# Gates of two routing groups in one pass behind the second list, constants and checks on other engines or later, u-term sums behind the mask

## The chip, the cores and the metric

The kernel runs on one core of a Trainium2 chip. The metric is the device time of one execution in microseconds (us); lower is better. A core has five engines, each with its own instruction stream: TensorE (PE, with its weight loads shown apart as PEld), VectorE (DVE), ScalarE (ACT), GpSimd (POOL) and SyncE (SP). They wait for one another by semaphores, and 16 DMA engines move the data.

## The reference

What is computed is a linear attention (4 batches, 8 heads, 768 steps, head size 48), whose output rows go through a mixture of 8 experts, two of them per token:

```python
for t in range(S):
    cur = np.einsum('bhd,bhe->bhde', u[None] * kt, vt)
    y[:, :, t] = np.einsum('bhd,bhde->bhe', rt, state + cur)
    state = w[None, :, :, None] * state + np.einsum('bhd,bhe->bhde', kt, vt)
x = y.transpose(0, 2, 1, 3).reshape(3072, 384)
noisy_logits = x @ w_gate + np.log1p(np.exp(x @ w_noise)) * noise
top2 = np.argpartition(-noisy_logits, 2, axis=1)[:, :2]
top2_w = softmax of the two logits, with 1e-9 in the denominator
for e in range(8):
    for k in range(2):
        mask = top2[:, k] == e
        h = np.maximum(x[mask] @ w1[e], 0.0)
        out[mask] += top2_w[mask, k, None] * (h @ w2[e])
```

Shapes of the experts: w1 is 8 x 384 x 1024, w2 is 8 x 1024 x 384, all float32.

## The kernel before

**Attention.** The 3072 tokens are 24 tiles of 128, i = chunk * 4 + batch. The loop `for i in range(NT)` writes each engine's stream in this order: `products(i)` puts the elementwise products on POOL (rku of tile i+1, L410 and L414, from tile 13 on L421 alone; kd of tile i+2, L402; the state's product z, L511); `ystate`, `kvup` and `yout` are matmuls into py and RV; `zup_v` folds RV into the state on DVE (z, L504 and L507); `uterm_b(i+1)` makes the "u-term" of the next tile on DVE: c, the sum of rku over a head (a reduce, L444; from tile 13 a copy, L442, of sums that PE makes from rku at L433 in the tile before), and, up to tile 8 (`CV_DVE`), cv = v * c (L448); `xout(i)` makes the tile's output x = py + cv (L560); `turn_kr(i+2)` transposes k and r on PE into KX and RV (L225), from which ACT makes kT (L462) and DVE rT (L464); `scores(i+1)` is 16 matmuls into PAB (L476); `turn_x(i)` transposes x (L225); and `mask(i+1)` makes am from PAB on DVE (L484, two instructions). RV is one buffer: the state's sums of tile i must have been read by z before `turn_kr(i+2)` may write it, and rT must have been read before the next sums.

**Routing.** Tiles 0 to 11 are group 0, tiles 12 to 23 group 1. `route(g)` turns a group's logits into the two chosen experts, each token's slot in its expert's list and its gates. It is a generator whose small DVE instructions are let in between the tiles by `steps` and `tick`: group 0 within tiles 13 to 23, group 1 within the first part of the expert stage. `drop` builds two operands on DVE (r_oa, r_ob) and queues a `place`, a set of matmuls (RT, L709) that scatters token numbers into a list; its `lag` says how many matmuls of the expert stage go ahead of it. `rows` turns the list L into gather indices (lt, lt, GR; L883 to L885), and `xgather` fetches the rows by indirect DMAs that POOL issues (L1020). `expneg` with the tag "r2" is a polynomial for exp, some 12 DVE instructions on 128 x 12 elements per group (L591 to L605); the gates follow (L842 to L854) and are written to DRAM by SP (xd<-r_a), from where the GT gathers read them. Within tiles 20 to 23, POOL also splits expert weights into high and low parts (w1l, L356 and L359).

**Experts.** Each list tile goes through ph = x w1 (L1131) and pym = h w2 (L1167), with every float32 matmul as three reduced-precision ones. `s` counts chunks of list tiles; `tile_counts` runs at s = 2.

**What sets the order.** The Python order above is each engine's instruction order; nothing is reordered later. A tile pool's buffer is free when its last reader is done.

Of the kernel before, what the change touches and what calls it, by code (L numbers as in the profile page):

```python
# [56 lines left out]
def kernel(  # L57
# [524 lines left out]
    def expneg(a, shape, tg, res):  # L582

        def T(nm, dt=F32):
            t = rtp[0].tile([128, GB * (E if len(shape) == 3 else 1)], dt, name=tg + nm, bufs=1)
# [83 lines left out]
    def drop(g, mm2, ej2, ijv, w_, c0, first):  # L669
# [29 lines left out]
        late_mm.append([2, lambda: place(n, parts, pL),  # L699
# [19 lines left out]
    def rest(g):  # L719
# [3 lines left out]
        for c in pairs(g, SLI[:, :, i0:i1], SL[g], "d"):  # L723
            yield 0.2
        mm2, ej2 = c
# [3 lines left out]
    GATES, list0 = {}, []  # L729

    def route(g, lists=True, behind=iter(())):
# [17 lines left out]
        for j, _ in enumerate(expneg(a, sh, "r1", ee)):  # L749
            if j == 1:  # L750
                nc.vector.tensor_add(zp, P(0, sh), gt)
            next(behind, None)
# [21 lines left out]
        for _ in behind:  # L774
            yield
# [3 lines left out]
        da, e2 = T("da", [128, n]), T("e2", [128, n])  # L779
# [24 lines left out]
        ex = expneg(da, [128, n], "r2", e2)  # L804
# [31 lines left out]
        if not lists:  # L836
            yield from slots(g, ex)
        def gates():
            for _ in ex:
                yield  # L840
            dn = GTS[:, 1, i0:i1]
            nc.vector.tensor_scalar(dn, e2, 1.0, 1e-9, op0=ALU.add, op1=ALU.add)  # L842
            yield
            gts = GTS[:, :, i0:i1]
            nc.vector.reciprocal(gts[:, 0], dn)
            yield
            nc.vector.tensor_mul(gts[:, 1], e2, gts[:, 0])
            yield
            if lists:
                og = T("os", [128, 2, n, E])  # L850
                nc.vector.tensor_mul(og, oh, gts[:, :, :, None].to_broadcast([128, 2, n, E]))
                yield 0.3
                gd = T("a")
                nc.vector.tensor_add(gd, og[:, 0], og[:, 1])  # L854
                while g and not list0:
                    yield "wait"
                nc.sync.dma_start(xd[i0 * 128:i1 * 128, DM:].rearrange("(n p) e -> p n e", p=128), gd)
                yield 0.25

        GATES[g] = gates()  # L860
        if not lists:
            yield from GATES[g]
        if lists:
# [23 lines left out]
    def tokens(a, b):  # L887
# [4 lines left out]
        f1 = const.tile([128, E * NJ], F32, name="f1")  # L892
# [123 lines left out]
    def xgather(e, ci, early_=-1):  # L1016
        for t in chunks(e)[ci]:
# [307 lines left out]
    for i in range(NT):  # L1325
        products(i)
        if early_done and (0, 0) not in XG:
            xgather(0, 0, 0)
        if i + 5 < NT:
            load(i + 5, (0, 2))  # L1330
        if i in (4, 6):
            next(flag)
        if NZ_AT <= i < NZ_AT + B:
            load_nz(i - NZ_AT)
        if i == B:
# [15 lines left out]
        if i and i + 1 < NT:  # L1351
# [6 lines left out]
        if i == I_EARLY and (0, 0) not in XG:  # L1358
            xgather(0, 0, 0)
        if i == NT - 1:  # L1360
            logits_out(i - 1)
            route_when_done(i - 1)
            steps(3)
            xT_first(lambda: turn_x(i))
            p1a = p1(0, 0)
        else:
# [11 lines left out]
            if not i:  # L1378
# [3 lines left out]
        if not i:  # L1382
# [87 lines left out]
    for s in range(1, len(seq)):  # L1470
# [96 lines left out]
        if s == 2:  # L1567
            tile_counts(CAP)
# [11 lines left out]
    with tc.If(any_r > 0):  # L1580
        bad_r = nc.values_load(tab[:, E:E + 1], min_val=0, max_val=1)
        with tc.If(bad_r > 0):
# [13 lines left out]
            nc.vector.memset(ie_n[:, 0, 0:1], 0.0)  # L1596
# [60 lines left out]
```

## Time and profile before

| | |
|---|---|
| median of 3 runs | 589.64 us (589.39 to 593.2) |
| the profiled execution | 589.92 us |
| its span, first to last instruction | 588.2 us |
| PE busy | 568.2 us (97%) |
| DVE / ACT / POOL busy | 348.1 (59%) / 284.5 (48%) / 280.0 us (48%) |
| mean granted clock of TensorE | 0.995 |
| chain that ended last | PE 89%, DVE 5%, POOL 2%, issue 2% |

The span is 1.72 us shorter than the profiled execution's time, and that execution is 0.28 us above the median. PE's share of 97% is a mean over two stages: the attention, up to about 128 us of the span, in which other engines hold PE at some places, and the experts behind it, in which PE is nearly always busy. In the rows below a time in brackets is the idle time of the engine before that instruction and what ended it. [...]

### The profile page before, as it was taken

Reading aid. Unit: us, or ns where it says so; the run is one execution under the profiler, and the core shown is the slowest. Engines: PE = TensorE matmul, PEld = TensorE weight load, DVE = VectorE, ACT = ScalarE, POOL = GpSimd, SP = SyncE. Lnnn points to the kernel's source line nnn. Section 1 sums busy time; section 2 is a strip of 40 time slices with the busy share of each in tenths; the row PEclk is TensorE's granted clock in tenths of the full one; section 3 lists DMA queues with packets and bytes.
Section 4 is the critical chain, followed back from the end, with each engine's and each line's share of the span. In section 5 each row is a group of like instructions: output and inputs, shape, how many; then the busy total and the mean of one; then the engine's idle time right before and its main releaser. Section 6 shows DMA issues by size and latency. Waiting matters only on the chain.

```text
span 588.2 us, 13907 instructions
## 1 busy us (share of the span) xinstructions
PE 568.2 (97%) x5383; PEld 543.4 (92%) x5384; DVE 348.1 (59%) x788; ACT 284.5 (48%) x712; POOL 280.0 (48%) x416
## 2 busy tenths in 40 slices
PE   8899899989999999999999999999999999999995
PEld 5799888879989999999999999999999999999995
DVE  7998698888864544556454554546363546454331
ACT  4348766842363624455445444454454455445220
POOL 8999455740336443436345453434262436423222
PEclk9999999989999999999999999999999999999999
DMA  8999889258405644765655646365845546424211
GB/s 166 224 219 205 201 202 210 83 142 258 125 35 189 184 131 120 189 138 175 108 154 164 177 116 200 98 184 127 173 118 153 169 127 187 124 82 85 67 35 42
DMA packets 143225, 86.53 MB, mean 147 GB/s; under 512 B 118624, under 2 KB 133215, under 8 KB 143152
## 3 DMA queue, kind: packets, MB, share of 16 engines
q1 hardware_dynamic: 132368, 56.76, 40.3%
q0 software_dynamic: 10160, 28.81, 16.0%
q8 instruction: 44, 0.72, 0.5%
q14 instruction: 29, 0.24, 0.1%
q10 hardware_dynamic: 624, 0.00, 0.1%
HBM read 58.81 MB, written 19.86 MB: 134 GB/s over the span
## 4 chain that ended last, share of the span: by engine, by line
PE 89%; DVE 5%; POOL 2%; issue 2%; ACT 1%; DMA 1%; POOLq 0%; ACTq 0%
PE ph L1131 37%; PE pym L1167 34%; PE py L531 4%; PE PAB L476 3%; PE pym L1160 2%; PE pym L1158 2%; PE KX L225 2%; PE py L569 1%; DVE am L484 1%; PE RV L494 1%; POOL kd L402 1%; PE RV L225 1%; PE RV L182 1%; PE RT L709 1%; PE ptm L1049 1%
## 5 line engine op out<-in xcount | busy, mean ns | idle before, releaser
L1167 PE MATMUL pym<-w1h,hb 128*128 128x384 f32 x768 | 200.3, 337 | 0.0
L1137 DVE SCALAR_TENSOR_TENSOR hb<-ph,hb 128x384 fp32r<-128x384 f32 x128 | 71.1, 556 | 116.7 <-ACT ht L1135 74.2
L1167 PEld LDWEIGHTS pym<-w1h,hb 128*128 128x128 f32 x768 | 139.3, 188 | 0.2
L1131 PE MATMUL ph<-xh,w0h 128*128 128x384 f32 (+1 forms) x384 | 136.0, 354 | 0.0
L1131 PE MATMUL ph<-xh,w0l 128*128 128x384 f32 (+1 forms) x384 | 135.6, 353 | 0.0
L1131 PE MATMUL ph<-xl,w0h 128*128 128x384 f32 (+1 forms) x384 | 130.4, 353 | 0.0
L1167 PE MATMUL pym<-w1l,hb 128*128 128x384 f32 x384 | 129.2, 336 | 0.0
L1135 ACT ACTIVATE hb<-ph 128x384 fp32r<-128x384 f32 x128 | 62.9, 492 | 106.7 <-PE ph L1131 106.7
L1192 POOL DMA_INDIRECT out_dram<-ot,TK x56 | 60.1, 1073 | 97.2 <-DVE ot L1186 42.1
L1020 POOL DMA_INDIRECT xg<-xd,GR x56 | 62.0, 1107 | 49.2 <-DVE r_e L603 24.4
L1131 PEld LDWEIGHTS ph<-xh,w0h 128*128 128x128 f32 x384 | 72.6, 189 | 3.5
L1131 PEld LDWEIGHTS ph<-xh,w0l 128*128 128x128 f32 x384 | 72.6, 189 | 3.1
L1131 PEld LDWEIGHTS ph<-xl,w0h 128*128 128x128 f32 x384 | 72.5, 189 | 3.2
L1035 POOL DMA_INDIRECT pv<-out_dram,GA x49 | 50.3, 1026 | 52.4 <-DMA out_dram<-ot,TK 39.7
L1167 PEld LDWEIGHTS pym<-w1l,hb 128*128 128x128 f32 x384 | 72.1, 188 | 0.1
L1105 ACT ACTIVATE xh<-xj 128x384 fp32r<-128x384 f32 (+1 forms) x42 | 21.1, 502 | 43.3 <-DVE xj L1103 43.1
L1175 ACT ACTIVATE ot<-pym 128x384 f32<-128x384 f32 x42 | 20.4, 486 | 39.9 <-PE pym L1167 33.1
L1106 DVE TENSOR_TENSOR xl<-xj,xh 128x384 fp32r<-128x384 f32 (+1 forms) x42 | 22.5, 535 | 24.8 <-ACT xh L1105 24.8
L1091 ACT ACTIVATE pl<-xg 128x768 uint16<-128x768 uint16 (+1 forms) x42 | 35.3, 841 | 1.4 <-DMA xd<-pl 1.4
L484 DVE TENSOR_TENSOR am<-PAB,mneg 128x512 int32<-128x512 int32 x48 | 30.8, 682 | 4.9 <-PE PAB L476 4.5
L476 PE MATMUL PAB<-rT,kT 64*128 64x128 f32 x384 | 27.7, 280 | 3.6 <-issue 3.2
L453 ACT ACTIVATE cv<-vt,c 128x48 f32<-128x48 f32 x120 | 30.2, 324 | 0.2
(276 smaller groups left out, 826.8 us busy)
## 6 DMA issues: line engine op xcount, KB each, us to landing
stg<-in_moe_w_dram SPq DMA_DIRECT2D x24, 512.0 KB, 4.7
stg<-in_moe_w_dram SPq DMA_DIRECT2D x32, 384.0 KB, 3.7
xd<-x SPq DMA_DIRECT2D x24, 196.0 KB, 3.3
rd<-in_r_dram SPq DMA_DIRECT2D x24, 192.0 KB, 4.3
vt<-in_v_dram SPq DMA_DIRECT2D x24, 192.0 KB, 4.3
out_dram<-ot SPq DMA_DIRECT2D x16, 288.0 KB, 4.1
kt<-in_k_dram SPq DMA_DIRECT2D x23, 192.0 KB, 3.8
xg<-xd,GR POOLq DMA_INDIRECT x56, 3.2
```

Of the source, the lines that this page charges most:

```text
L453: nc.scalar.activation(CV[i][:, h, :], vt[i][:, h, :], AF.Copy, scale=C8[i][:, h, :])
L476: nc.tensor.matmul(pa[:, s, p, :], kT[i][s * 64:(s + 1) * 64, p, :], rT[i][s * 64:(s + 1) * 64, p, :], start=True, stop=True)
L484: nc.vector.tensor_tensor(am[:, :, h].bitcast(I32), pa[:, :, h].bitcast(I32), mneg[:, None].to_broadcast([128, 2, NP // 2, 128]), op=ALU.b ...
L531: nc.tensor.matmul(o[qs], lhsT[:, qs], rhs, start=first[q], stop=last, skip_group_check=True)
L1020: nc.gpsimd.indirect_dma_start(out=xg[:n, :XW if e else DM], out_offset=None, in_=xd[:rows_of(early_)], in_offset=bass.IndirectOffsetOnAxi ...
L1035: nc.gpsimd.indirect_dma_start(out=pv[:n], out_offset=None, in_=out, in_offset=bass.IndirectOffsetOnAxis(ap=GA[:n, e * NJ + t:e * NJ + t + ...
L1091: nc.scalar.activation(pl[:n], XG[e, t][:n, :DM].bitcast(U16).rearrange("p (d two) -> p two d", two=2), AF.Copy)
L1131: nc.tensor.matmul(ph[:, :w_], a[:, d, fs], x[:, d, :w_], start=(j == 0), stop=(j == len(q) - 1))
L1135: nc.scalar.activation(h_[:, f, 0, :], ph[:, a:b], AF.Relu)
L1137: nc.vector.scalar_tensor_tensor(h_[:, f, 1, :], ph[:, a:b], 0.0, h_[:, f, 0, :].bitcast(F32), op0=ALU.max, op1=ALU.subtract)
L1167: nc.tensor.matmul(py, hb[:, f, a, hs], x[:, f, :], start=(j == 0), stop=(j == len(q) - 1))
L1192: st = nc.gpsimd.indirect_dma_start(out=out, out_offset=bass.IndirectOffsetOnAxis(ap=TK[:n, q:q + 1], axis=0), in_=ot[:n], in_offset=None, ...
```

## The change

- `consts_v`: two constants, ltri and ie_n, are made by ACT in tile 5 instead of by DVE in tile 0; ieu is made only where a fallback needs it.
- The two pieces of `consts_c`, a check of the inputs' range on DVE with one matmul, move from tiles 4 and 6 to s = 2 of the experts, ahead of `tile_counts`. A POOL memset (`consts_b`) moves from tile 4 to tile 10.
- `uterm_b(i+1)` of tiles 1 to 7 moves from ahead of `xout(i)` to behind `mask(i+1)`.
- Behind `xout`, `maybe_early` may now run: `rows` of group 0 comes directly behind x of tile 21, and the first of three gathers is issued there, the other two in tile 22.
- The "r2" instructions leave `route`. One pass over 24 columns, `gates((0, 1))`, runs behind the second list; both writes xd<-r_a follow it. In `route(1)`, `rest_pre(0)` (slots and pairs of group 0) now fills the place of group 1's first "r2" instructions. The place of the second list has lag 3.
- Not shown in the diff: larger "r2" tiles, and a scratch tile of the checks that shares a buffer.

```diff
     def consts_v():
-        nc.vector.tensor_scalar(ltri, idif, 0.0, None, op0=ALU.is_gt)
-        nc.vector.tensor_copy(ieu, ie)
-        nc.vector.tensor_scalar(ie_n[:, 0, :], ie, float(LS), None, op0=ALU.mult)
+        nc.scalar.activation(ltri, mneg[:, 0, :], AF.Copy, scale=-1.0)
+        nc.scalar.activation(ie_n[:, 0, :], ie, AF.Copy, scale=float(LS))
...
-        late_mm.append([2, lambda: place(n, parts, pL),
+        late_mm.append([lag, lambda: place(n, parts, pL),
...
+
+    def rest_pre(g):
         i0, i1 = GROUPS[g]
         yield from slots(g)
         yield 0.2
-        for c in pairs(g, SLI[:, :, i0:i1], SL[g], "d"):
+        for PRE[g] in pairs(g, SLI[:, :, i0:i1], SL[g], "d"):
             yield 0.2
-        mm2, ej2 = c
+
+    def rest(g):
+        if g not in PRE:
+            yield from rest_pre(g)
+        mm2, ej2 = PRE[g]
         for kk in range(2):
             yield from drop(g, mm2[:, kk], ej2[:, kk], IJ_REST, (E - 1) * NJ, NJ, g == 0 and kk == 0)
-    GATES, list0 = {}, []
...
+
+    def gates(gs, lists=True):
+
+        i0, i1 = GROUPS[gs[0]][0], GROUPS[gs[-1]][1]
+        e2 = rtp[0].tile([128, NT], F32, name="r_e2", bufs=1)[:, :i1 - i0]
+        dn = GTS[:, 1, i0:i1]
+        yield from expneg(dn, [128, i1 - i0], "r2", e2)
+        nc.vector.tensor_scalar(dn, e2, 1.0, 1e-9, op0=ALU.add, op1=ALU.add)
+        yield
+        nc.vector.reciprocal(GTS[:, 0, i0:i1], dn)
+        yield
+        nc.vector.tensor_mul(dn, e2, GTS[:, 0, i0:i1])
+        yield
+        for g in gs if lists else ():
+            i0, i1 = GROUPS[g]
+            n = i1 - i0
+            T = T_of(n)
+            og = T("os", [128, 2, n, E])
+            nc.vector.tensor_mul(og, OHS[g], GTS[:, :, i0:i1, None].to_broadcast([128, 2, n, E]))
+            yield 0.3
+            gd = T("a")
+            nc.vector.tensor_add(gd, og[:, 0], og[:, 1])
+            while not list0:
+                yield "wait"
+            nc.sync.dma_start(xd[i0 * 128:i1 * 128, DM:].rearrange("(n p) e -> p n e", p=128), gd)
+            yield 0.25
...
         for _ in range(3):
-            next(ex, None)
+            next(behind, None)
+            next(behind, None)
             yield
...
-            yield from GATES[g]
+            yield from slots(g)
+            for _ in gates((g,), False):
+                pass
...
                 yield 0.2
-            yield from drop(g, *c, IJ_0, NJ, 0, g == 0)
+            yield from drop(g, *c, IJ_0, NJ, 0, g == 0, 3 if g else 2)
         routed.add(g)
-        if lists and not g:
-            while not early_done:
-                yield "wait"
-            for c in GATES[0]:
-                yield c
...
-                route_q.append(route(g))
+                route_q.append(route(g, True, rest_pre(0) if g else iter(())))
...
         products(i)
-        if early_done and (0, 0) not in XG:
-            xgather(0, 0, 0)
+        if early_done and (0, 2) not in XG:
+            xgather(0, 0, 0, [t for t in chunks(0)[0] if (0, t) not in XG])
         if i + 5 < NT:
             load(i + 5, (0, 2))
-        if i in (4, 6):
-            next(flag)
         if NZ_AT <= i < NZ_AT + B:
             load_nz(i - NZ_AT)
-        if i == B:
+        if i == 10:
...
-        if i and i + 1 < NT:
+        if CV_DVE <= i < NT - 1:
             uterm_b(i + 1)
         steps(1)
         xout(i)
         while i == I_EARLY and not early_done:
             rstep(1)
             maybe_early()
-        if i == I_EARLY and (0, 0) not in XG:
-            xgather(0, 0, 0)
+        maybe_early()
+        if early_done and (0, 0) not in XG:
+            xgather(0, 0, 0, chunks(0)[0][:1 if i < I_EARLY else 3])
         if i == NT - 1:
             logits_out(i - 1)
             route_when_done(i - 1)
-            steps(3)
...
             mask(i + 1)
-            if not i:
+            if i < CV_DVE:
                 uterm_b(i + 1)
             steps(3)
             maybe_early()
-        if not i:
+        if i == 5:
             consts_v()
...
     def rest_0():
         def gates_0():
-            yield from GATES[1]
+            yield from gates((0, 1))
...
         if s == 2:
+            for _ in flag:
+                pass
             tile_counts(CAP)
```

**DVE, tiles 1 and 2** (rT, am: the operands of PE's next work; c, cv: the u-term; z: the state; x: the output). Before, from rT of tile 2 to x of tile 1:

```order
L464 TENSOR_TENSOR rT<-RV,pwr 128x2x4x64
L484 TENSOR_TENSOR am<-PAB,mneg 128x2x256 x2
L444 TENSOR_REDUCE c_406<-rku 128x8
L448 TENSOR_TENSOR cv<-vt,c_406 128x384
L310 TENSOR_SCALAR ltri<-stg 128x128
L311 CAST ieu<-ie 128x8
L312 TENSOR_SCALAR ie_n<-ie 128x8
L504 TENSOR_TENSOR z_215<-RV,w_176 128x192
L444 TENSOR_REDUCE c_457<-rku 128x8
L448 TENSOR_TENSOR cv<-vt,c_457 128x384
L560 TENSOR_TENSOR x_147<-py,cv 128x384
```

With the change, from rT of tile 2 to rT of tile 3:

```order
L463 TENSOR_TENSOR rT<-RV,pwr 128x2x4x64
L483 TENSOR_TENSOR am<-PAB,mneg 128x2x256 x2
L443 TENSOR_REDUCE c_406<-rku 128x8
L447 TENSOR_TENSOR cv<-vt,c_406 128x384
L503 TENSOR_TENSOR z_215<-RV,w_176 128x192
L559 TENSOR_TENSOR x_147<-py,cv 128x384
L463 TENSOR_TENSOR rT<-RV,pwr 128x2x4x64
```

The three constants are gone from ahead of z, and the second c and cv from ahead of x.

**POOL, tiles 21 to 23** (rku: the products of the next tile's u-term; kd: k scaled; w1l: a weight's low part; xg: gathered rows). Before:

```order
L421 TENSOR_TENSOR rku<-rT,kT 128x256 x2
L402 TENSOR_TENSOR kd_101<-kt,tabk 128x4x48 x2
L359 TENSOR_TENSOR w1l_1337<-stg,w1h_1336 128x384
L421 TENSOR_TENSOR rku<-rT,kT 128x256 x2
L1020 DMA xg<-xd,GR 128x384 x3
L356 TENSOR_TENSOR w1l_1337<-stg,w1h_1336 128x384
L359 TENSOR_TENSOR w1l_1337<-stg,w1h_1336 128x384
```

With the change:

```order
L420 TENSOR_TENSOR rku<-rT,kT 128x256 x2
L401 TENSOR_TENSOR kd_101<-kt,tabk 128x4x48 x2
L1019 DMA xg<-xd,GR 128x384
L358 TENSOR_TENSOR w1l_1327<-stg,w1h_1326 128x384
L420 TENSOR_TENSOR rku<-rT,kT 128x256 x2
L1019 DMA xg<-xd,GR 128x384 x2
L355 TENSOR_TENSOR w1l_1327<-stg,w1h_1326 128x384
L358 TENSOR_TENSOR w1l_1327<-stg,w1h_1326 128x384
```

The first xg moved ahead of one w1l and of the last rku.

**DVE, group 1's list** (hb: the experts' activations; r2t, r_e, r2r, r2s: the exp; r_os to r_dm: slots and pairs of group 0; r_s to SLF: slots of group 1). Before:

```order
L1137 SCALAR_TENSOR_TENSOR hb<-ph,hb 128x384 x2
L591 TENSOR_SCALAR r2t<-r_da 128x12
L593 TENSOR_SCALAR r_e_3100<-r2t 128x12
L595 SCALAR_TENSOR_TENSOR r2r<-r_e_3100,r_da 128x12
L596 TENSOR_SCALAR r2s<-r2t 128x12
L827 TENSOR_SCALAR r_s_3192<-RT 128x1
L829 TENSOR_TENSOR ie_n<-ie_n,r_s_3192 128x1
L830 TENSOR_TENSOR acc<-acc,r_sm 128x8
L834 TENSOR_TENSOR SLF_245<-RT,ie_n 128x96
```

With the change:

```order
L1136 SCALAR_TENSOR_TENSOR hb<-ph,hb 128x384 x2
L640 TENSOR_TENSOR r_os<-OH_242,SLF_244 128x192
L644 TENSOR_REDUCE r_sl<-r_os 128x24
L648 CAST SLI<-r_sl 128x2x12
L658 TENSOR_SCALAR r_dj<-SLI 128x24
L663 CAST r_de_3156<-r_dj 128x48
L665 SCALAR_TENSOR_TENSOR r_dm_3155<-r_dj,r_sl 128x48
L854 TENSOR_SCALAR r_s_3160<-RT 128x1
L856 TENSOR_TENSOR ie_n<-ie_n,r_s_3160 128x1
L857 TENSOR_TENSOR acc<-acc,r_sm 128x8
L861 TENSOR_TENSOR SLF_245<-RT,ie_n 128x96
```

Six instructions of group 0 stand where four of group 1's exp stood, ahead of group 1's slots.

## Rows read from the trace of the kernel before

**Rows 1.** Busy time by stretch: us, busy (instructions) by engine, clock, DMA

```profile
12.49:44.18 31.69, 29.05 (x757) 27.26 (x755) 30.01 (x60) 12.66 (x34) 30.66 (x52) 1.00 0.97 218
...
66.72:72.87 6.15, 4.73 (x128) 4.53 (x126) 3.25 (x9) 3.86 (x13) 2.98 (x5) 1.00 0.76 163
...
128.42:132.00 3.58, 3.58 (x16) 3.58 (x13) 2.28 (x11) 0.47 (x2) 0.00 (x0) 0.52 0.97 250
```

**Rows 2.** VectorE timeline, tiles 1 to 4: start us, us, engine, line, tiles

```profile
15.98 0.61 DVE L310 TENSOR_SCALAR ltri<-stg 128x128 bf16<-128x128 int32 x1
...
17.07 0.34 DVE L504 TENSOR_TENSOR z<-RV,w 128x192 f32<-128x192 f32 x1
...
18.23 0.90 DVE L448 TENSOR_TENSOR cv<-vt,c 128x384 f32<-128x384 f32 x1
...
22.14 0.60 DVE L448 TENSOR_TENSOR cv<-vt,c 128x384 f32<-128x384 f32 x1
...
23.90 1.29 DVE L484 TENSOR_TENSOR am<-PAB,mneg 128x512 int32<-128x512 int32 x2
...
27.91 1.27 DVE L484 TENSOR_TENSOR am<-PAB,mneg 128x512 int32<-128x512 int32 x2
```

**Rows 3.** TensorE timeline, tiles 1, 7 and 8

```profile
17.47 0.46 PE L225 MATMUL RV<-ident,rd 64*128 64x64 f32 x8 [1.23 <-DVE z L504]
...
44.18 1.11 PE L476 MATMUL PAB<-rT,kT 64*128 64x128 f32 x16
...
48.40 1.11 PE L476 MATMUL PAB<-rT,kT 64*128 64x128 f32 x16
```

**Rows 4.** GpSimd timeline, tiles 1 and 2

```profile
16.47 1.13 POOL L414 TENSOR_TENSOR rku<-rku,ub 128x192 f32<-128x192 f32 x2
...
20.08 1.14 POOL L414 TENSOR_TENSOR rku<-rku,ub 128x192 f32<-128x192 f32 x2
```

**Rows 5.** Waits of ScalarE, first 50 us: us in total, times, longest

```profile
ACT kT L462 <- PE KX L225: 13.1, 9, 2.0
```

**Rows 6.** VectorE timeline, tiles 21 to 23

```profile
115.83 0.56 DVE L560 TENSOR_TENSOR x<-py,cv 128x384 f32<-128x384 f32 x1
...
118.97 0.17 DVE L885 TENSOR_SCALAR GR<-lt 128x3 int32<-128x3 f32 x1
...
122.41 2.72 DVE L603 SCALAR_TENSOR_TENSOR r_e<-r_e,r2r 128x12 f32<-128x12 f32 x2
```

**Rows 7.** GpSimd timeline, tiles 21 to 23

```profile
115.06 1.00 POOL L359 TENSOR_TENSOR w1l<-stg,w1h 128x384 fp32r<-128x384 f32 x1
117.29 1.43 POOL L421 TENSOR_TENSOR rku<-rT,kT 128x256 f32<-128x256 f32 x2 [1.23 <-DVE rT L464]
119.43 1.15 POOL L1020 DMA_INDIRECT xg<-xd,GR  x1 [0.71 <-DVE r_e L600]
...
123.12 1.02 POOL L356 TENSOR_TENSOR w1l<-stg,w1h 128x384 fp32r<-128x384 f32 x1
```

**Rows 8.** TensorE timeline, end of the attention

```profile
118.97 0.60 PE L433 MATMUL py<-uw,rku 128*64 128x2 f32 x16
...
122.62 1.09 PE L531 MATMUL py<-vt,am 128*64 128x48 f32 x32
...
126.56 0.40 PE L225 MATMUL KX<-ident,x 64*128 64x64 f32 x6 [1.75 <-DVE x L560]
```

**Rows 9.** VectorE timeline, second list

```profile
149.06 0.17 DVE L885 TENSOR_SCALAR GR<-lt 128x4 int32<-128x4 f32 x1
...
149.63 0.35 DVE L641 TENSOR_TENSOR r_os<-OH,SLF 128x192 f32<-128x192 bf16 x1
```

**Rows 10.** TensorE timeline, second list and the next tile

```profile
148.13 0.29 PE L709 MATMUL RT<-r_ob,r_oa 128*128 128x16 bf16 x6 [0.48 <-ACT r_ob L700]
...
153.29 0.49 PE L1049 MATMUL ptm<-ident,xg 128*128 128x128 f32 x3
```

**Rows 11.** DMA issues (page): operation, count, KB each where shown, median us to landing

```profile
xg<-xd,GR POOLq DMA_INDIRECT x56, 3.2
```

More of the change, by code (lines that the diff above doesn't have):

```diff
@@ L584, in T @@
         def T(nm, dt=F32):
-            t = rtp[0].tile([128, GB * (E if len(shape) == 3 else 1)], dt, name=tg + nm, bufs=1)
+            t = rtp[0].tile([128, GB * E if len(shape) == 3 else NT], dt, name=tg + nm, bufs=1)
             if len(shape) == 2:
@@ L667, in pairs, with drop @@
         yield mm2, ej2
-    def drop(g, mm2, ej2, ijv, w_, c0, first):
+    def drop(g, mm2, ej2, ijv, w_, c0, first, lag=2):
         i0, i1 = GROUPS[g]
@@ L717, in placed @@
             nc.vector.tensor_add(Lv, Lv, pL[:, :, :w_])
-    def rest(g):
+    PRE = {}
+    def rest_pre(g):
         i0, i1 = GROUPS[g]
@@ L722, in rest @@
         yield 0.2
-        for c in pairs(g, SLI[:, :, i0:i1], SL[g], "d"):
+        for PRE[g] in pairs(g, SLI[:, :, i0:i1], SL[g], "d"):
             yield 0.2
-        mm2, ej2 = c
+    def rest(g):
+        if g not in PRE:
+            yield from rest_pre(g)
+        mm2, ej2 = PRE[g]
         for kk in range(2):
             yield from drop(g, mm2[:, kk], ej2[:, kk], IJ_REST, (E - 1) * NJ, NJ, g == 0 and kk == 0)
-    GATES, list0 = {}, []
+    list0 = []
+    def gates(gs, lists=True):
[22 more added lines that the diff above has]
+            yield 0.25
     def route(g, lists=True, behind=iter(())):
@@ L751, in route @@
                 nc.vector.tensor_add(zp, P(0, sh), gt)
-            next(behind, None)
             yield
@@ L768, in route @@
             nc.vector.scalar_tensor_tensor(q, q, cc, s2, op0=ALU.add, op1=ALU.mult)
-            next(behind, None)
             yield
@@ L773, in route @@
         nc.vector.tensor_add(nl, q, zp)
-        for _ in behind:
-            yield
         yield
@@ L778, in route @@
         OHS[g] = oh
-        da, e2 = T("da", [128, n]), T("e2", [128, n])
+        da = GTS[:, 1, i0:i1]
         if lists:
@@ L836, in route @@
         if not lists:
[L837 to L855, printed above, removed]
-                    yield "wait"
[L857 to L861, printed above, removed]
-            yield from GATES[g]
+            yield from slots(g)
+            for _ in gates((g,), False):
+                pass
         if lists:
@@ L870, in route @@
                 yield 0.2
-            yield from drop(g, *c, IJ_0, NJ, 0, g == 0)
+            yield from drop(g, *c, IJ_0, NJ, 0, g == 0, 3 if g else 2)
         routed.add(g)
-        if lists and not g:
-            while not early_done:
-                yield "wait"
-            for c in GATES[0]:
-                yield c
     def rows(a, b, n=N):
@@ L891, in tokens @@
         f0 = const.tile([128, E * NJ], F32, name="f0")
-        f1 = const.tile([128, E * NJ], F32, name="f1")
+        f1 = const.tile([128, E * NJ], F32, name="lt", bufs=2)
         nc.vector.tensor_scalar(ti[:, :w_], L[:, 0, a:b], -1.0, 0.0, op0=ALU.add, op1=ALU.max)
@@ L1014, in rows_of, with xgather @@
         return GROUPS[g][1] * 128
-    def xgather(e, ci, early_=-1):
-        for t in chunks(e)[ci]:
+    def xgather(e, ci, early_=-1, ts=None):
+        for t in ts or chunks(e)[ci]:
             n = tw(t)
@@ L1596 @@
             nc.vector.memset(ie_n[:, 0, 0:1], 0.0)
+            nc.vector.tensor_copy(ieu, ie)
             for i in range(NT):
```

1 line of the change is left out of this document (removed).

## The prediction

> **What bounds the kernel now.** I read the table of times first, then the busy time by stretch, then waits and timelines of the stretches that the change touches. PE is busy for 97% of the span, and the chain of waits is 89% PE: the experts, from about 180 us on, are PE's own work, and the change takes no matmul out of it. So a gain can only come from places in which PE idles or runs slowly, and there are few. In the stretch from the scores of tile 1 to those of tile 8, PE is busy 29.05 of 31.69 us [rows 1]: 2.64 us are idle, and DVE (30.01) and POOL (30.66) are nearly full, so an engine that feeds PE sets the pace there. [...] At the second list PE waits again, by about half a microsecond at a place [rows 10].
>
> **The early tiles: 2.5 us gained (1.3 to 3.0).** Before z of tile 1, DVE makes the three constants: they begin at 15.98 and z at 17.07, and PE's transposes into RV wait 1.23 us for that z [rows 2, 3]. Without them z comes 1.09 us earlier. The moved c and cv do the rest: x of a tile no longer stands behind the next tile's sums and so behind POOL's rku. What is left on DVE in a tile is mask, c, cv, z, x and rT, and such a round was 4.01 us from tile 3 to tile 4 (27.91 less 23.90, the masks) [rows 2]. PE's pace where it is the bound is 4.22 (48.40 less 44.18) [rows 3]. Of the seven intervals from 12.49 to 44.18, three at DVE's round (12.3 together, the first somewhat over 4.01) and four at 4.22 (16.9) make 29.2 where 31.69 stood: 2.5. Removing the range checks from tiles 4 and 6 is part of that sum. PE's idle 2.64 and a little of tile 0 give the upper bound, 3.0.
>
> The round now has c and cv in series with z, since z stands behind them on DVE, and PE's transposes wait for z. Two things can lengthen it. First, c needs POOL's rku: it ends at 17.60 and 21.22, 3.62 apart [rows 4], while DVE, by rounds of 4.01 to 4.1, reaches c at 18.95 and 23.0 by my estimate, so POOL stays ahead. Second, cv took 0.60 at one place and 0.90 at another [rows 2], beside POOL's work. If each of the first three tiles is hit by 0.4, counting c, then 1.2 of the gain goes: 1.3 is left, the lower bound. I take 2.5, since the slower cv is the rarer one and POOL, ahead of need, has less to do beside it later.
>
> [...]
>
> ltri and ie_n cost ACT two short instructions: nothing, as ACT waits 13.1 us for PE's transposes in the first 50 us [rows 5]. The memset moves beside POOL's pauses: nothing. Should that cover go, each is under half a microsecond.
>
> **The end of the attention: 0.7 us gained (0 to 2.3).** Removed are group 0's exp and gates between tiles 21 and 23. Two such r_e instructions on 12 columns took 2.72 us at 122.41, where others took about 0.17 each: they ended at 125.13, when POOL's two w1l (1.02 from 123.12, and a like one behind it) were done [rows 6, 7]. Behind them stood the last x, although PE's y of tile 23 was done at 123.71 (122.62 and 1.09) [rows 8]. With x right behind y, PE's transposes of it could come after 124.3 instead of 126.56.
>
> But POOL's order is new. The first gather now stands ahead of a w1l and of the last rku. x of tile 21 ends at 116.39; three small instructions of 0.17 to 0.2 make GR at 116.95; the gather then takes 117.2 to 118.35 (its row 1.15), w1l 1.00 and rku 1.43, so rku ends at 120.75 with POOL's gaps [rows 6, 7]. Before, it ended at 118.72, because w1l ran at 115.06 and only rT held rku [rows 7]; PE needs it at 118.97 [rows 8]. PE would now stop for 1.75 us there, and y of tile 23 ends at 125.46. x follows (0.56), the transposes start at 126.1, and less of DVE's and ACT's work stands behind them: I put the first expert matmul at 127.75 against 128.42, 0.7 earlier. Bounds: if PE's stop costs all that the blocked r_e cost, 0; if rku is there in time, 2.3.
>
> **The clock: 1.7 us gained (0 or 1.7).** 3.58 us at 0.52 lose 3.58 x 0.48 = 1.7. Ahead of them PE had idled 1.75 at one place and about half a microsecond once more. In the stretch 66.72 to 72.87 it idled 1.42 of 6.15 us, and the granted clock stayed 1.00 [rows 1]. With the change the longest pause just ahead of the experts is about 0.5, and the 1.75 lies 8 us earlier. So I expect the clock to stay, at three chances in four.
>
> **The second list: 0.7 us lost (2.5 lost to 0.9 gained).** Six instructions of group 0's slots now stand ahead of group 1's, where four of 0.17 stood. Six cost between 6 x 0.17 = 1.0 and 6 x 0.35 = 2.1 [rows 9]; at 1.4 the operands of the list come about 0.8 later. The lag of 3 puts that place's matmuls later by as much, so PE's wait of 0.48 [rows 10] stays. Seven instructions of the new gate pass stand between the operands and the sum of the list: 7 x 0.19 = 1.3. GR, which was at 149.06, comes 1.3 to 1.4 later. Its gather lands 3.2 after issue [rows 11], that is at about 152.7 before and 154.0 now, and PE's ptm needs it at 153.29 [rows 10]: 0.7 late. The two later places see their operands earlier in one case and later in the other; I let that cancel. If two more places wait by 0.9 each, 2.5 is lost; if both known waits vanish and the gather is in time, 0.9 is gained. The writes xd<-r_a and the gathers of gates come later; these stand behind on SP and POOL, and nothing on PE needs them for many microseconds.
>
> **The checks at s = 2: 0.1 lost (0 to 0.5).** DVE is half idle among the experts. PE has one more small matmul there and may wait for its operand; the nearest row is the 0.48 at the list [rows 10].
>
> **The sum.** 2.5 + 0.7 + 1.7 - 0.7 - 0.1 = 4.1. From the profiled execution, 589.92, that gives 585.8. The median of the runs is 0.28 below that execution; that is inside their spread, and I leave the forecast at 585.8.
>
> **Rivals.**
> (a) The forecast with its smaller terms, 584.5 to 587.2: 0.46.
> (b) The clock falls all the same: 585.8 + 1.7 = 587.5. For it speaks that PE still pauses twice in its last tiles. 0.13.
> (c) rku comes in time, or POOL's stop is covered, and the list costs nothing: up to 1.6 and 0.7 better, 583.5, in a span of 582 to 584.5. It decides by when GR is written: 1.7 us earlier than I reckon would do. 0.22.
> (d) The early tiles give their gain back because something else than DVE sets their pace: 588.3. DMA was at 0.97 of its capacity in that stretch; and between 66.72 and 72.87 PE idles 1.42 in one pause for which the trace shows no other engine, which returns about every 256 instructions (128 matmuls and 126 weight loads here) [rows 1]. If loads, of data or of code, were late by the clock on the wall and not by the count of tiles, work done sooner would only wait. 0.09. [...]
> (e) Slower: c waits for POOL's rku in tiles 1 to 8, and z and the transposes with it. It decides when POOL needs more per tile than DVE and PE, that is over 4.2 where 3.62 is shown [rows 4]. At 4.8, seven tiles lose 7 x 0.6 = 4.2 and the gain of 2.5 is lost: 592.5. 0.06.
> (f) The moves change nothing that PE waits for: 589.9. 0.04.
>
> **Numbers.** The forecast is 585.8. The range 582.0 to 588.8 holds (a) to (d) and leaves out (e), (f) and tails of (c) and (d), 0.15 or so. About 1% is what a measurement of this kernel can tell from no change, and the three runs spread by 0.6% already. Faster by over 1%, under 583.74: most of (c) and the low edge of (a), 0.19. Slower by over 1%, over 595.5: a piece of (e), 0.03. Within: 0.78.
>
> **What would show it.** Right: the scores of tile 8 at about 41.7 and no wait of the transposes for z; a wait of PE of about 1.7 at the u-term sums of tile 22, ended by POOL's rku; the last x directly behind y; the granted clock at 1.00 as the experts begin; a span near 584. Wrong: c idle on rku in tiles 2 to 8; waits at PAB that grow by what the tiles gained; a slow stretch at the start of the experts; ptm waits over 1 us for xg around 154.

## The result, and the profile after

The changed kernel takes 597.72 us (median of 6 runs, 595.4 to 600.84), the kernel before 590.66 beside it (6 runs, 589.39 to 593.24). The ratio is 1.0113, with a 95% interval of 1.0072 to 1.0154: slower by 1.1%. The forecast was 585.8 with a range up to 588.8: the sign was wrong.

The head of the page of after, whose profiled execution took 598.3 (before: 589.92):

```profile
span 596.5 us, 13894 instructions
...
PE 573.1 (96%) x5383; PEld 546.3 (92%) x5384; DVE 343.8 (58%) x770; ACT 284.6 (48%) x714; POOL 274.5 (46%) x416
```

The span grew from 588.2 to 596.5, by 8.3. To find where, I cut both spans at events that both traces have: the first `ph` (first expert matmul), the first `pym`, and the first matmul of the second expert tile's `pym`. The TensorE timeline of after (start us, us, line, tiles, and in brackets the idle time ahead and what ended it):

```profile
16.75 0.46 PE L225 MATMUL RV<-ident,rd 64*128 64x64 f32 x8
...
43.03 1.11 PE L475 MATMUL PAB<-rT,kT 64*128 64x128 f32 x16
...
120.90 0.40 PE L432 MATMUL py<-uw,rku 128*64 128x2 f32 x8 [0.95 <-POOL rku L420]
...
121.57 0.40 PE L432 MATMUL py<-uw,rku 128*64 128x2 f32 x8 [0.27 <-POOL rku L420]
...
128.13 0.40 PE L225 MATMUL KX<-ident,x 64*128 64x64 f32 x6 [0.20 <-DVE x L559]
...
129.99 0.44 PE L1130 MATMUL ph<-xh,w0h 128*128 128x384 f32 x1
...
143.21 0.42 PE L1166 MATMUL pym<-w1h,hb 128*128 128x384 f32 x1
...
153.87 0.55 PE L1048 MATMUL ptm<-ident,xg 128*128 128x128 f32 x3 [0.26 <-DMA xg<-xd,GR]
...
161.59 0.43 PE L708 MATMUL RT<-r_ob,r_oa 128*128 128x100 bf16 x6 [3.10 <-DVE r_ob L691]
...
162.97 0.43 PE L708 MATMUL RT<-r_ob,r_oa 128*128 128x100 bf16 x6 [0.95 <-DVE r_sl L644]
...
184.97 0.34 PE L1166 MATMUL pym<-w1h,hb 128*128 128x384 f32 x1
```

| stretch | before | after | difference |
|---|---|---|---|
| start to first `ph` | 128.42 | 129.99 | +1.57 |
| first `ph` to first `pym` (143.14; 143.21) | 14.72 | 13.22 | -1.50 |
| first `pym` to the second tile's (176.96; 184.97) | 33.82 | 41.76 | +7.94 |
| from there to the end of the span | 411.24 | 411.53 | +0.29 |

Nearly all of it lies in the stretch in which the second list is made, beside the first expert tile. There PE waits 3.10 and 0.95 at the two halves (x6 each) of a place of 100 columns, where before it waited at none of that size; its waits at the place of 16 columns ahead are much the same (0.64 and 0.49, before 0.44 and 0.48 [rows 10]). The windows of after (the columns of [rows 1]) show what follows the pause, and two other stretches:

```profile
12.86:43.03 30.17, 29.21 (x756) 27.31 (x754) 27.42 (x50) 13.00 (x36) 29.37 (x51) 1.00 0.91 199
...
122.41:126.30 3.89, 3.89 (x54) 3.77 (x52) 1.92 (x4) 2.33 (x9) 2.69 (x4) 0.56 0.53 157
130.00:149.20 19.20, 18.07 (x126) 17.61 (x123) 17.24 (x72) 4.99 (x12) 0.00 (x0) 1.00 0.80 246
...
158.00:163.20 5.20, 1.14 (x16) 0.86 (x15) 2.69 (x10) 1.37 (x3) 0.00 (x0) 1.00 0.37 32
163.20:170.34 7.14, 6.72 (x26) 5.74 (x22) 3.55 (x12) 0.81 (x3) 4.84 (x5) 0.52 0.56 211
```

From 158.00 to 163.20 PE is idle for 4.06 us; then the granted clock, as a share of full speed, is 0.52 for 7.14 us (the `ph` begin 0.37 apart in it, and 0.20 from 170.54 on): 7.14 x 0.48 = 3.4 lost. The two waits and the clock make 7.5 of the 7.94.

Who was late is on VectorE. Its timeline in after, one early row and then the second list:

```profile
62.70 0.55 DVE L443 TENSOR_REDUCE c<-rku 128x8 f32<-128x384 f32 x1 [2.34 <-POOL rku L413]
...
155.62 0.25 DVE L756 TENSOR_TENSOR r_a<-r_os 128x96 f32<-128x96 f32 x1
...
156.52 0.31 DVE L691 TENSOR_TENSOR r_ob<-r_de,ij 128x300 bf16<-128x300 bf16 x1
160.41 0.26 DVE L756 TENSOR_TENSOR r_a<-r_os 128x96 f32<-128x96 f32 x1 [3.58 <-DMA xd<-r_a]
160.59 0.31 DVE L694 TENSOR_TENSOR r_ob<-r_ob,thi 128x300 bf16<-128x300 bf16 x1
```

ACT finishes that `r_ob`:

```profile
160.99 0.54 ACT L699 ACTIVATE r_ob<-r_ob,pcol 128x300 bf16<-128x300 bf16 x1 [3.71 <-DVE r_ob L694]
```

and SP's queue in after (two writes joined in one row; the second was issued at 160.70):

```profile
157.77 3.32 SPq L759 DMA_DIRECT2D xd<-r_a  x2
```

L756 adds the two gates of a group into a tile `T("a")`, which has one buffer. The first add, for group 0, ends at 155.87. Its write to memory is issued at 157.77 and must have read the tile before the second add, for group 1, may overwrite it. So DVE stands 3.58 us at that add, and the next `r_ob` (L694), behind it in DVE's order, begins only at 160.59. ACT's part of that `r_ob` (L699) can only follow, and ends at 161.53; PE's list place starts at 161.59. (PE's row names an L691 instead, which ends at 161.58: that one stands behind L694 on DVE and is for the second half.) Before, group 0's add stood at 126.80 and its write at 127.08, group 1's add at 151.91: the same buffer cost nothing, 25 us apart.

The early part, on POOL's timeline in after:

```profile
47.63 1.15 POOL L401 TENSOR_TENSOR kd<-kt,tabk 128x192 f32<-128x192 f32 x2 [2.09 <-DMA kt<-in_k_dram]
...
117.96 1.15 POOL L1019 DMA_INDIRECT xg<-xd,GR  x1 [2.04 <-DVE GR L884]
119.15 1.01 POOL L358 TENSOR_TENSOR w1l<-stg,w1h 128x384 fp32r<-128x384 f32 x1
120.11 1.41 POOL L420 TENSOR_TENSOR rku<-rT,kT 128x256 f32<-128x256 f32 x2
```

The scores of tiles 1 to 8 took 30.17 where 31.69 stood [rows 1], and those of tile 8 came at 43.03 instead of 44.18 [rows 3]: 1.15 ahead, because the scores of tile 1 began 0.37 later (12.86, before 12.49). Then the lead goes. Scores of tile 10 come at 52.0 (before 52.6), of tile 12 at 61.2 (61.1), of tile 22 at 117.0 (116.2). From 37 us on, POOL's kd waits for loads of k three times, 3.4 us in all, and VectorE's c three times for POOL, 3.9 in all; the trace of before has no wait for k, and of c for POOL one of 0.2. The longest wait of c, 2.34 at 62.70, follows a kd that began 1.36 late at 58.38; the trace of after puts that to PE, those of two later versions put the same kd's 1.82 and 1.91 to the load of k.

### The profile page after: what moved, and what is told of

Its sections match the earlier page's. It is cut to its first block, busy times and chain, and to the rows that moved or that the text cites. A ratio compares the mean times of both kernels' runs of the same rounds, so it can differ in the third digit from the quotient of the medians.

```text
span 596.5 us, 13894 instructions
## 1 busy us (share of the span) xinstructions
PE 573.1 (96%) x5383; PEld 546.3 (92%) x5384; DVE 343.8 (58%) x770; ACT 284.6 (48%) x714; POOL 274.5 (46%) x416
## 4 chain that ended last, share of the span: by engine, by line
PE 80%; issue 6%; POOL 4%; DVE 4%; DMA 3%; ACT 1%; SPq 0%; POOLq 0%; DVEq 0%; ACTq 0%
PE ph L1130 35%; PE pym L1166 32%; PE py L530 3%; PE PAB L475 2%; PE pym L1157 2%; PE pym L1159 2%; POOL kd L401 1%; PE KX L225 1%; POOL rku L409 1%; DMA kt<-in_k_dram 1%; DVE am L483 1%; POOL rku L413 1%; DVE x L559 1%; PE RV L182 1%; PE py L432 1%
## 5 line engine op out<-in xcount | busy, mean ns | idle before, releaser
L1191 POOL DMA_INDIRECT out_dram<-ot,TK x56 | 57.8, 1032 | 106.3 <-DVE ot L1185 50.6
L1130 PEld LDWEIGHTS ph<-xh,w0l 128*128 128x128 f32 x384 | 72.5, 189 | 3.1
L1166 PEld LDWEIGHTS pym<-w1l,hb 128*128 128x128 f32 x384 | 72.5, 189 | 0.1
L1034 POOL DMA_INDIRECT pv<-out_dram,GA x49 | 48.2, 983 | 45.4 <-DMA out_dram<-ot,TK 31.1
L1104 ACT ACTIVATE xh<-xj 128x384 fp32r<-128x384 f32 (+1 forms) x42 | 21.1, 502 | 44.2 <-DVE xj L1102 43.9
L475 PE MATMUL PAB<-rT,kT 64*128 64x128 f32 x384 | 28.9, 286 | 2.2 <-issue 1.8
L401 POOL TENSOR_TENSOR kd<-kt,tabk 128x192 f32<-128x192 f32 x46 | 28.1, 631 | 5.6 <-DMA kt<-in_k_dram 3.4
```

The source lines that it names most:

```text
L401: nc.gpsimd.tensor_mul(KD[i][:, h], kt[i][:, h], tabk[:, h, :D])
L475: nc.tensor.matmul(pa[:, s, p, :], kT[i][s * 64:(s + 1) * 64, p, :], rT[i][s * 64:(s + 1) * 64, p, :], start=True, stop=True)
L1034: nc.gpsimd.indirect_dma_start(out=pv[:n], out_offset=None, in_=out, in_offset=bass.IndirectOffsetOnAxis(ap=GA[:n, e * NJ + t:e * NJ + t + ...
L1130: nc.tensor.matmul(ph[:, :w_], a[:, d, fs], x[:, d, :w_], start=(j == 0), stop=(j == len(q) - 1))
L1166: nc.tensor.matmul(py, hb[:, f, a, hs], x[:, f, :], start=(j == 0), stop=(j == len(q) - 1))
L1191: st = nc.gpsimd.indirect_dma_start(out=out, out_offset=bass.IndirectOffsetOnAxis(ap=TK[:n, q:q + 1], axis=0), in_=ot[:n], in_offset=None, ...
```

## The experiments

My theory had three parts: the shared buffer costs the stretch of the list; late loads of k take the early gain back; and six slot instructions ahead of the list cost more than I gave them. Each was taken out on top of the mended buffer, then all together; the first gather went back behind rku on the way. "Ratio" is to the kernel before, measured beside it; before had medians of 592.01, 592.02, 592.11 and 592.36 in the four series (35, 29, 27 and 17 runs).

### A buffer of its own

```diff
-            gd = T("a")
+            gd = T("a" if g else "nl")
```

> The changed kernel, with one difference: the second group's expert gates are added into r_a and the first group's into another idle buffer (r_nl), so that the second add does not wait for the first group's write to DRAM. Theory A (the shared buffer is what costs): in the changed kernel DVE stood 3.58 us in front of that add, with the operands of the next list place behind it, TensorE waited 3.10 and 0.95 us at the places, and then ran 7.14 us at a granted clock of 0.52 (3.4 us lost). All of this goes: about 4.0 + 3.4 = 7.4 us less, 590.3 against 597.7, and no wait of TensorE over 0.7 us at a place. Rival B (the list is late because of the six instructions and the seven of the gate pass ahead of it): those stay, so no more than 1 us is won, 596.5 or above, and the places still wait.

592.94 us, ratio 0.9997 (0.9972 to 1.0022). Span 591.2. VectorE and TensorE at the same places (timelines of this kernel):

```profile
157.58 0.25 DVE L756 TENSOR_TENSOR r_a<-r_os 128x96 f32<-128x96 f32 x1
```

```profile
160.13 0.43 PE L708 MATMUL RT<-r_ob,r_oa 128*128 128x100 bf16 x6 [0.55 <-DVE r_sl L644]
```

The second add no longer waits, PE's 3.10 has become 0.55, and the stretch between the `pym` is 35.43 where 41.76 stood. By the ratios one buffer is the whole slowdown; it isn't yet a gain, and that stretch is still 1.61 longer than before. In this trace the granted clock fell elsewhere, to 0.5 over 65.7 to 72.5, behind a pause of 1.38.

### The u-term sums in their old place

```diff
-        if CV_DVE <= i < NT - 1:
+        if i and i + 1 < NT:
...
-            if i < CV_DVE:
+            if not i:
```

> As e1_own_buffer, with the u-term sums (c, cv) of tiles 1 to 7 back ahead of x of the tile before; constants and checks stay moved. Theory A (the early gain of 1.15 us at tile 8 is lost again by tile 12, as loads come late): within 0.5 us of e1_own_buffer, or up to 1 us faster. Rival B (the move is worth what it shows at tile 8): 1.0 to 1.5 us slower than e1_own_buffer.

Made on top of the version with the buffer of its own: 593.03, ratio 1.0016 (0.9993 to 1.0038), against 0.9997 with the sums moved. The intervals overlap: moving them is worth 0.002 at the most likely, and nothing that is settled. In the one trace of each, the scores of tile 8 come at 46.04 with the sums back and at 42.72 without, those of tile 12 at 63.57 and 61.46, so of a lead of 3.3 there are 2.1 left at tile 12, where theory A had it lost. At tile 22 (118.86 and 119.06) it is gone: in between lies the fall of the clock at 65.7 that only the version with the sums moved had.

### The u-term sums alone

> The kernel before, with only the u-term sums of tiles 1 to 7 moved behind the mask. Theory A (DVE gives time in the early tiles, but loads of k come late and take it back before tile 13): 589.5 to 591.5, that is no change, with scores of tile 8 earlier by about 1 us and those of tile 12 not. Rival B (the gain is kept): 588.0 to 589.3.

The kernel before with only that move (the diff above, reversed): 593.4, ratio 1.0022 (1.0001 to 1.0043). Scores of tile 8 come at 43.9 (before 44.2), of tile 12 at 62.1 (61.1), and kd waits 1.8 us for k, which it did not before. So the first tiles gain 0.3 and the next ones lose 1.3.

### The first gather back behind rku

```diff
-        if early_done and (0, 0) not in XG:
-            xgather(0, 0, 0, chunks(0)[0][:1 if i < I_EARLY else 3])
+        if i == I_EARLY and (0, 0) not in XG:
+            xgather(0, 0, 0)
```

> As e1_own_buffer, with the first early gather back behind the last rku on GpSimd; the indices (GR) are still made directly behind x of tile 21. Theory A (the gather ahead of rku stops TensorE 1.22 us at the u-term sums and lowers its clock to 0.56 for 3.89 us, a loss of 1.7): both go, 2.0 to 2.9 us faster than e1_own_buffer, and the granted clock stays at 1.00 from 118 us to the experts. Rival B (the end of the attention hangs on the last gathers as much): the gather of the first rows lands later and the transposes of them wait, within 0.5 us of e1_own_buffer.

On top of the own buffer: 590.83, ratio 0.9979 (0.9957 to 1.0001). PE's wait at L432 is gone, and the clock is 1.00 in the last tiles. Windows of this kernel:

```profile
119.00:123.31 4.31, 4.31 (x117) 4.17 (x115) 2.84 (x8) 3.36 (x12) 2.60 (x4) 1.00 0.12 47
123.31:129.74 6.43, 5.60 (x119) 4.71 (x116) 3.52 (x8) 4.61 (x16) 4.22 (x5) 1.00 0.58 172
```

From the scores of tile 22 to the first `ph` it takes 10.25 us, where 13.0 stood in after and 12.2 before. But the version from which it was made took 11.63: there the same pause stood, and the clock did not fall behind it:

```profile
122.97 0.40 PE L432 MATMUL py<-uw,rku 128*64 128x2 f32 x8 [0.95 <-POOL rku L420]
```

```profile
122.97:127.00 4.03, 3.75 (x82) 3.36 (x84) 1.93 (x4) 1.68 (x7) 3.54 (x4) 1.00 0.35 98
```

So the gather ahead of rku costs 1.4 in that stretch by these two traces, about the pause itself, and 2.8 against after, where a slow clock came with it. In the times the gain over the version before it (0.9997) is inside the intervals.

### The slots of group 0 back behind the list

```diff
-                route_q.append(route(g, True, rest_pre(0) if g else iter(())))
+                route_q.append(route(g))
```

> As e3_gather_back, with the six instructions of group 0's slots and pairs back behind the second list, so that only the gate pass stands there. In e3_gather_back the stretch from the first matmul with w2 to the second group's first (142.96 to 178.32) takes 35.36 us, before the change 33.82. Theory A (the six instructions ahead of group 1's slots make the list late): 0.6 to 1.0 us shorter in that stretch, 0.1 to 0.2% faster. Rival B (the later places wait because the gate pass stands among their operands): the later places wait for operands that now are made behind the list, 0.5 us or more longer.

On top of the last: 589.0, ratio 0.9941 (0.9918 to 0.9964). The places of the list stand on PE without a wait:

```profile
147.49 0.46 PE L708 MATMUL RT<-r_ob,r_oa 128*128 128x16 bf16 x12
...
154.62 0.69 PE L708 MATMUL RT<-r_ob,r_oa 128*128 128x100 bf16 x12
```

The stretch between the `pym` is 33.04, against 35.36 with the six instructions ahead: they cost 2.3 us, more than either theory had. In the times the intervals (0.9979 before this step) just overlap. The stretch is also 0.78 below that of before; whether the one gate pass or the lag of 3 makes that, no run separates.

### Loads a tile earlier

```diff
-NV = 6
-NK = 6
+NV = 7
+NK = 7
...
+    load(5, (0, 2))
...
-        if i + 5 < NT:
-            load(i + 5, (0, 2))
+        if i + 6 < NT:
+            load(i + 6, (0, 2))
```

> As e3_gather_back, with k and r of a tile loaded one tile earlier (seven buffers of each where there were six). Theory A (the loads are late because they are asked for late): GpSimd's waits for k (4.4 us in e3_gather_back between tiles 8 and 13) go, the scores of tile 22 come 2 to 3 us earlier, and the time is 588 to 589, 0.3 to 0.5% below e3_gather_back. Rival B (the DMA engines are full, 0.97 of their capacity in that stretch, so that asking earlier brings nothing): the waits stay or move, and the time is within 0.2% of e3_gather_back.

On top of the version with the first gather back: 587.66, ratio 0.995 (0.9912 to 0.9987); the interval overlaps that of 0.9979, so it is the trace that shows the gain. The same stretch of time, in the version without the earlier loads and then in this one:

```profile
8.00:66.00 58.00, 52.66 (x1303) 49.22 (x1305) 48.46 (x90) 30.58 (x90) 50.30 (x85) 0.97 0.90 194
```

```profile
8.00:66.00 58.00, 55.81 (x1435) 52.34 (x1435) 52.08 (x98) 35.01 (x104) 53.02 (x91) 1.00 0.96 206
```

PE does 1435 matmuls instead of 1303 in the same 58 us, one tile more: at 66 us it makes the scores of tile 13, where those of tile 12 stood. Part of it is the clock: the version without the earlier loads ran at 0.50 from 61.20 to 64.50, behind a pause of 2.11 for an x whose DVE had stood 2.88 at c for rku. No kd waits for k in tiles 1 to 13; the scores of tile 22 come at 114.59 instead of 119.49, and the first `ph` at 124.96 instead of 129.74.

### Fewer loads of v

```diff
-            load(i + 4, (2, 3))
+            if 6 <= i + 4 < 14:
+                vt[i + 4] = vt[i]
+            else:
+                load(i + 4, (2, 3))
```

> As e3_gather_back, but v of tiles 6 to 13 is not loaded: those tiles use v of tile 2 to 5 again, so that the output is another one and the experts get other tokens; only the stretch up to the experts is to be read. It takes some 25% of the traffic out of tiles 2 to 9. Theory A (the loads set the pace of tiles 8 to 13): no wait of GpSimd for k, scores of tile 12 at or before 60 us and of tile 22 at 114 to 116.5 us (119.5 in e3_gather_back). Rival B (something else than loads holds these tiles): tile 22 at 118 us or later though no load is late.

A single run, with the v of tiles 6 to 13 left out (older tiles stand in for it), so only the attention is read: no wait for k, scores of tile 12 at 60.6, of tile 22 at 112.7, first `ph` at 122.98, tile 22 earlier than theory A had it. Here fewer bytes did what earlier loads did: tile 22 came at 112.7 with the one and at 114.59 with the other.

### The noise on ScalarE's queue

```diff
-        nc.sync.dma_start(nz[:, :, b, :], ...
+        nc.scalar.dma_start(nz[:, :, b, :], ...
```

> As e3_gather_back, with the four loads of the noise (768 rows of 32 bytes each, tiles 5 to 8) issued by ScalarE and not by SyncE. Theory A (SyncE issues in order, and a load of noise that takes it up to 3.2 us holds the next loads of v and k): k lands earlier, GpSimd's waits for it shrink by half or more, 0.2 to 0.4% faster than e3_gather_back. Rival B (the DMA engines are the bound, whoever issues): no change beyond 0.2%, waits for k still 3 us or more in all.

591.96, ratio 0.999 (0.9967 to 1.0014), no better than the 0.9979 of the version that it was made from. The waits of kd for k shrank to 1.2, as theory A has it, but the time did not follow. The trace is of the slowest of its 13 runs (597.36): ScalarE, with the noise now on its queue, stood 2.31 ahead of one zb and 5.17 ahead of another, at 42.03; PE waited 3.57 for the kT behind that, and then ran at 0.50 from 43.45 to 49.30. So the move cost elsewhere, and how much of k's lateness is its place on SP's queue stays open.

### Earlier loads alone, and all mends together

> The kernel before, with k and r loaded one tile earlier and nothing else. Theory A (before the change DVE sets the pace of the early tiles and the loads are just in time, so that earlier loads bring little): 0.998 to 1.000. Rival B (late loads cost the kernel before as well, in most of its runs): 0.994 to 0.997.

The kernel before with the earlier loads only: 593.06, ratio 1.0019 (0.9991 to 1.0048). In before nothing waits for k, so bringing it sooner brings nothing.

> e9_slots_back and e11_load_earlier together: own buffer, gather behind rku, group 0's slots behind the list, k and r loaded one tile earlier. If the parts are independent, the ratios add: 0.9941 and 0.995/0.9979 give 0.991, about 586.7. If the earlier loads only fitted the one order (rival), no better than 0.994.

All three mends and the earlier loads on the change: 588.39, ratio 0.9917 (0.9882 to 0.9952): 0.8% under before, and 1.9% under the change by the two ratios (0.9917 / 1.0113 = 0.981). The parts added up would give 0.991, so they are independent as far as these runs tell. Its timeline on TensorE:

```profile
124.86 0.44 PE L1130 MATMUL ph<-xh,w0h 128*128 128x384 f32 x1
...
138.08 0.42 PE L1166 MATMUL pym<-w1h,hb 128*128 128x384 f32 x1
...
171.11 0.34 PE L1166 MATMUL pym<-w1h,hb 128*128 128x384 f32 x1
```

The first `ph` is 3.56 before that of the kernel before, and the stretch between the `pym` is 33.03. This version beats both kernels.

> As e12_all_mended, with the u-term sums of tiles 1 to 7 back ahead of x of the tile before. Theory A (with the loads in time, moving the sums is worth what was forecast for the early tiles, 2.5 us less the part of the constants, 1.1): 1.0 to 1.5 us slower than e12_all_mended, 0.2%. Rival B (it is worth nothing even then): within 0.1% of e12_all_mended.

With the u-term sums back in their old place: 588.46, ratio 0.9942 (0.9912 to 0.9972). Against 0.9917 the intervals overlap and the medians agree. The one trace of each differs, though: with the sums back the first `ph` comes at 127.52 instead of 124.86, 2.66 later. It comes from the stretch between the scores of tiles 2 and 3, which takes 7.21 instead of 4.19; there x stands behind c, which waits 1.32 for rku:

```profile
20.13 0.58 PE L225 MATMUL KX<-ident,x 64*128 64x64 f32 x6 [1.95 <-DVE x L559]
```

```profile
20.13:23.00 2.87, 2.87 (x54) 2.75 (x54) 2.83 (x6) 1.17 (x4) 2.87 (x6) 0.50 0.80 155
```

That the move of the sums gains in most runs once the loads are early stays unsettled.

### The shared buffer put back into the mended version

```diff
-            gd = T("a" if g else "nl")
+            gd = T("a")
```

> The kernel with all three mends, with one of them taken out again: both groups' gates are added into the one buffer r_a. In the mended kernel the two adds stood at 147.23 and 148.36 us, and the write of the first was issued at 151.16 and lands some 2.7 later. Theory A (the shared buffer holds DVE, and with it the operands of PE's list places): the second add waits from about 148.4 to 153.9, 5.5 us, with r_ob, r_oa and xl behind it; PE stands by over 2 us near 150 to 156, and the stretch from the first pym to the second stretch of pym is 38 to 42 us where 33.03 stood; the ratio to the kernel before rises from 0.992 to between 1.000 and 1.008. Theory B (the difference of 1.2% between the change and its version with a buffer of its own came mostly from where the granted clock happened to fall, and from the spread of runs): the second add waits, but the stretch stays under 35.5 us and the ratio under 0.996.

596.43, ratio 1.0038 (1.0005 to 1.0072), against 0.9917 (0.9882 to 0.9952): 1.2%, some 7 us, for the name of one tile. VectorE, and TensorE at the place of the list:

```profile
159.31 0.26 DVE L756 TENSOR_TENSOR r_a<-r_os 128x96 f32<-128x96 f32 x1 [5.34 <-DMA xd<-r_a]
```

```profile
160.48 0.66 PE L708 MATMUL RT<-r_ob,r_oa 128*128 128x100 bf16 x6 [5.09 <-ACT r_ob L699]
```

The first add is at 152.75 and its write issued at 156.66; DVE stands 5.34 us and PE 5.09, after which the granted clock is 0.50 from 160.50 to 165.00. The stretch between the `pym` is 40.38 where 33.03 stood, inside the 38 to 42 expected. In this run kd waited for k again, three times and 3.3 us in all, although the loads were early. Its span is 13.0 longer than that of the mended version; 5.5 of that lie ahead of the first `ph`, where the edit changes nothing, and 7.35 in the stretch between the `pym`, which fits the 7 us of the ratios.

## Why the prediction was wrong

**The failed step** is one sentence of the second list: "The writes xd<-r_a and the gathers of gates come later; these stand behind on SP and POOL, and nothing on PE needs them for many microseconds." It is true of the data. But I followed only who reads what the write writes, not who must wait until the write has read. Both groups' sums go into the one buffer r_a, the change brought them from 25 us to about 1 apart, and the order rows of VectorE would have shown an r_ob between and behind them. Sized from what after shows, the term was 3.1 to 4 of waiting and 3.4 of clock; taken out and put back, it was worth 1.2% twice. None of the rivals, and not the one on the slower side, named it. With that one buffer mended the change comes out at 0.9997, which is no change at all. So the other terms, 4.1 together, did not arrive either:

**The early tiles** (2.5 forecast, 1.3 to 3.0). z no longer waits: PE's transposes into RV come at 16.75 without a wait, where 1.23 stood [rows 3]. At tile 8 the lead was 1.15, under my lower bound; the stretch from tile 1 itself was 1.52 shorter, inside the range. Neither part of the move does it alone: by the traces that stretch took 31.69 before, 31.47 with only the sums moved, 33.54 and 32.18 with all but the sums moved, and 29.78 to 30.33 with both (the change 30.17, its own buffer 30.33, all mends 29.78). What I feared for cv didn't happen where I feared it: in tiles 1 to 4 it took 0.61 to 0.62 each time, with POOL busy 29.37 of 30.17 us [first row of the windows above], and of the first nine in after only two, at 32.58 and 41.42, took 1.05 and 0.99; why those two, no run shows. What took the lead was the loads half of rival (d), to which I gave 0.09: with work done sooner, k was not there, POOL's kd waited 2.09 at 47.63, and c behind it (0.78 at 51.95). From tile 8 on, c of the next tile stands ahead of x on VectorE, so the wait reaches PE. I had its evidence, DMA's busy share of 0.97 [rows 1], and treated it as the least of it. The other half of (d), code, no run tests: pauses of PE that the trace puts to no engine stand there between 66 and 97 us in both (0.49 to 1.42 before, 0.54 to 1.21 after); the first three of each stand 252 to 254 matmuls and weight loads apart.

**The end of the attention** (0.7 forecast). PE's stop at the u-term sums came as worked out, of the size 0.95 + 0.27 = 1.22 instead of 1.75, ended by POOL's rku behind the gather and w1l. (My rows add up to 120.78 for the end of rku, not 120.75; it ended at 121.52.) The last x did stand right behind y: its wait was 0.20 where 1.75 stood [rows 8]. But the first `ph` came 13.0 after the scores of tile 22 instead of 12.2, because of the next term: in the version with its own buffer, where the same stop stood and the clock held, it took 11.6, which is 0.6 less than before and near the 0.7 forecast.

**The clock** (1.7 forecast). The experts did start at 1.00, and that stretch is 1.50 shorter. But the 1.22 pause had its own drop right behind it: 0.56 over 3.89 us, which loses 3.89 x 0.44 = 1.7. I had written that the pause lay 8 us earlier, and took that as its being harmless: in this trace the loss moved, it did not go. In the version with its own buffer the same pause was followed by none, so the term hangs on more than the pause, and no run here says on what.

**The second list** (0.7 lost). GR's lateness was right: it came 1.24 later (150.30), where I had 1.3 to 1.4, and ptm waited 0.26 for xg, where I had 0.7. The six instructions were forecast at 0.8 and cost 2.3 in the stretch, near the end of the range (2.5): in the version without them PE waits at none of the list's places, with them three times (0.65, 0.48 and 0.55 in the trace with the first gather back), and for an xh besides (0.42).

The checks among the experts were priced rightly at next to nothing: from the second `pym` on the difference is 0.29. No run takes them out by themselves, nor the constants on ACT, the memset or the lag of 3.

What stays open: the mended version's runs fall into two groups of five, 583.28 to 586.94 and 589.84 to 590.46, so that its median, 588.39, lies between them and is no run's time. Whether it is the loads, as the wait for k in the last experiment may suggest, or the place at which the clock falls, no run here separates.

## What to carry to other kernels

When a change brings two uses of a tile near each other, list for each tile its buffers and everything that must have read the old content, DMA writes included. Here VectorE stood 3.58 and 5.34 us at the second use, and the price was that of what stood behind it: PE's waits of 3.10 and 5.09 at the list, and the clock that fell behind them, 3.4 in after. Where a stretch is made faster, look at what feeds it: here the loads of k, for which nobody waited before and kd waited 3.4 us in after, ate the gain by the traces until they were issued a tile earlier, and issuing them earlier without the gain was worth nothing (ratio 1.0019). A pause that is moved is not a pause removed; here the clock fell to 0.56 behind it in the change, and stayed at 1.00 in the version with its own buffer.

## What the runs showed of the hardware

The granted clock fell to about half (0.50 to 0.56 in the windows above) in 12 of the 14 traces, behind different pauses: over 3.89 us behind 1.22 in after, over 7.14 behind 4.06, over 6.8 behind 1.38 in the version with its own buffer. It did not fall behind pauses of about 0.5 at the list (0.44 and 0.48 in before, 0.64 and 0.49 in after, at 1.00 each time). A pause of 1.42 in the attention of before [rows 1] was not followed by a drop, nor was the 0.95 and 0.27 at the u-term sums in the version with its own buffer, which in after was; so the length of the last pause alone does not tell. In two traces, the first with earlier loads and that with fewer loads of v, it did not fall ahead of the end at all.

The write of one r_a (128x96 f32) to memory held its buffer for 2.64 us from its issue in after (157.77 to 160.41) and for 2.65 in the last experiment (156.66 to 159.31). The rest of the add's wait was time in which the write had not yet been issued.
